# A list-scheduled transformer block: the scheduler's durations, tails and semaphore latencies set to figures read from a profile

## The chip, the cores and the metric

Each kernel runs on one core of a Trainium2 chip. Runs 1 to 4 below were taken on one chip, 5 to 8 on a second and 9 to 12 on a third, each time with the kernel before in the same rounds (medians 871.2, 870.7 and 871.7). The time is device microseconds (us) from the first to the last instruction, the median of several executions. All runs compared here are of the fast state. Ratios are the mean time of one kernel's fast runs over the mean of the other's of the same rounds, so they are not quite the ratio of the medians quoted. A profile is one execution; its span is 1 to 3 us shorter than the time of the run.

The clock granted to PE varies a little among runs of the fast state, and the time goes with it: in the rounds of runs 1 to 4 the kernel before took 869.85 to 870.05 us at a mean clock of 1.000 and 877.17 at 0.987. Most runs below had 0.996 to 1.000, so by my estimate from these figures (7.2 us for 0.013) some 2 us of a difference between two kernels can be the clock's.

The engines in the profile's lines: PE (matrix multiplication), PEld (its weight load), ACT (ScalarE), DVE (VectorE), POOL (GpSimd).

## The reference

A transformer block on 2048 tokens of width 512: layer norm, attention with 32 heads of 16, a residual, layer norm, a gated feed-forward part of width 1792, a residual.

```python
h  = x + mha(layernorm(x), wqkv, wo)           # 32 heads, Dh = 16, softmax over 2048 keys
h2 = h + (gelu(n @ w_gate) * (n @ w_up)) @ w_down      # n = layernorm(h)
```

Attention dominates: 2048 tiles of scores, 128 keys by 512 query columns each, and each needs an exponential (759.2 of ACT's 803.3 busy us in the profile of before, and DVE's conversions another 275.4 on DVE).

## The kernel before

All instructions are put in order when the program is built. Each part of the work (scores, exponentials, products with V, projections, feed-forward) is a stream of operations with a planned duration. A greedy scheduler keeps a clock for each engine and always emits the operation that can start first by that clock. Each engine gets its own list of instructions in that order, with semaphores for the true dependences. So by design a planned duration can't make a wrong result (two experiments, 8 and 12, did give one, with the look-ahead and the tail reserve moved); it only changes order, and one choice described below.

When may an operation start, by the plan?

```python
            if op.eng == "pe":
                lag = LAT + (SLACK if op.writes[0] in SOFT else 0.0)      # LAT = 0.12
                return max([self.done[t] + lag for t in toks if t[0] != "pe"] + [0.0])
            ...
            self.done[tok] = end + (PLAG if op.mode != "f" else 0.0)      # PLAG = 0.02
```

The exponential of a tile can be had in two ways. ACT takes two tiles per instruction (1024 columns, two banks of `pbank`, double-buffered):

```python
            yield Op("act", 0.093 + 0.427 * n, ACTF(PT[...], pbank[:, b0:b0 + n, :], ACT.Exp, ...), ...)
```

DVE takes single tiles. It converts each one to 16 bits, and finishes a group of four with two bit operations and one product:

```python
    def dconv(G, j, b):
        yield Op("dve", 0.7, lambda e: e.tensor_scalar(out=dXE..., in0=pbank[:, b, :], ...), ...)
    def dchain(G):
        t1, t2 = 0.16 + 0.133 * n, 0.16 + 0.267 * n      # n = 4 tiles
        yield Op("dve", t1, ...)                         # W: mantissa
        yield Op("dve", t1, ...)                         # E: exponent
        yield Op("dve", t2, ...)                         # product
```

A tile has no fixed engine. While the program is built, a new DVE group is opened whenever the plan of DVE is less than 0.8 us ahead (and the ring of four buffers has room, and 3 us have passed):

```python
        def room():
            if C["gopen"] or ... or sch.t["dve"] > sch.now + 0.8:
                return False
            ...
            return sch.now >= C["dnext"] + (DBUSY if C["down"] < first_t[C["cdone"]] else 0)
```

So planned durations decide how many tiles DVE gets. That is the one choice besides order.

Dense matmuls (projections, feed-forward) go between the scores, if they end no later than a limit before the next scores are due:

```python
        due = self.due = max(q[0][0], self.t["act"] - QLEAD)              # QLEAD = 0.5
        ok = [... if s.head.mode == "q" or max(self.t["pe"], r) + s.head.dur + ... <= due + QTOL]   # QTOL = 0.2
```

## Time and profile before

| | before |
|---|---|
| time, median (range) | 871.05 us (870.17 to 871.24, 4 runs) |
| span of the profile | 869.4 us |
| ACT exponentials / DVE conversions | 816 / 417 |

The prediction below shows the page's main lines. Here are the lines behind one term of its account: a visit of ACT to the gelu table, in order of time (start, duration, engine, line, operation, tiles).

```profile
307.07 1.28 ACT L1809 ACT_TABLE_LOAD   x1
308.37 6.27 ACT L1809 ACTIVATE GUT<-GUT 128x3584 bf16<-128x3584 bf16 x2
314.65 1.28 ACT L1278 ACT_TABLE_LOAD   x1
315.95 7.56 ACT L1278 ACTIVATE PT<-pbank 128x1024 bf16<-128x1024 f32 x8
```

From the first load to the next exponential: 315.95 - 307.07 = 8.88 us in which ACT makes no exponential. Such a visit isn't idle time, so it must be a term of its own.

The waits (who waited for whom: us in total, times, longest):

```profile
DVE dXE L1590 <- PE pbank L1272: 58.9, 122, 1.4
...
ACT PT L1278 <- PE pbank L1272: 22.4, 32, 9.0
PEld pbank L1272 <- DVE dXE L1590: 15.4, 47, 0.4
```

DVE waits four times as long for PE as PE's scores and products wait for DVE's conversions: DVE has room. The third line is the one to watch when DVE is filled.

### The profile page before, as it was taken

Reading aid. Unit: us, or ns where it says so; the run is one execution under the profiler, and the core shown is the slowest. Engines: PE = TensorE matmul, PEld = TensorE weight load, DVE = VectorE, ACT = ScalarE, POOL = GpSimd, SP = SyncE. Lnnn points to the kernel's source line nnn. Section 1 sums busy time; section 2 is a strip of 40 time slices with the busy share of each in tenths; the row PEclk is TensorE's granted clock in tenths of the full one; section 3 lists DMA queues with packets and bytes.
Section 4 is the critical chain, followed back from the end, with each engine's and each line's share of the span. In section 5 each row is a group of like instructions: output and inputs, shape, how many; then the busy total and the mean of one; then the engine's idle time right before and its main releaser. Section 6 shows DMA issues by size and latency. Waiting matters only on the chain.

```text
span 869.4 us, 16682 instructions
## 1 busy us (share of the span) xinstructions
PE 840.3 (97%) x6781; PEld 255.7 (29%) x6781; DVE 735.0 (85%) x1177; ACT 803.3 (92%) x853; POOL 42.2 (5%) x100
## 2 busy tenths in 40 slices
PE   8999999999999989999999989999999989999987
PEld 4222222222222222222222222222233333334445
DVE  7669999999879989899988989889888898589842
ACT  2799999999999999999999999999999999999941
POOL 4700000000010000000020000000000000000000
PEclk9999999999999999999999999999999999999999
DMA  6000005200000000000000000000000000000000
GB/s 194 1 1 1 1 2 199 69 1 2 2 12 1 2 1 1 13 25 2 1 13 2 1 1 1 13 26 1 1 26 2 2 1 2 8 26 8 2 13 18
DMA packets 12328, 15.06 MB, mean 17 GB/s; under 512 B 1745, under 2 KB 11217, under 8 KB 12241
## 3 DMA queue, kind: packets, MB, share of 16 engines
q1 hardware_dynamic: 12240, 13.90, 4.8%
q8 instruction: 55, 0.90, 0.4%
q14 instruction: 33, 0.26, 0.1%
HBM read 11.80 MB, written 2.10 MB: 16 GB/s over the span
## 4 chain that ended last, share of the span: by engine, by line
PE 70%; ACT 20%; issue 6%; DVE 3%; POOL 0%; ACTq 0%; DVEq 0%; POOLq 0%
PE pbank L1272 43%; PE pbank L1271 20%; ACT PT L1278 18%; PE pbank L1870 4%; ACT GUT L1809 1%; PE pbank L1867 1%; PE pbank L1275 1%; ACT L1278 1%; PE pbank L1880 1%; DVE VA L1428 1%; PE pbank L1747 0%; DVE stats L1344 0%; DVE dXE L1590 0%; PE pbank L1725 0%; DVE QT L1416 0%
## 5 line engine op out<-in xcount | busy, mean ns | idle before, releaser
L1278 ACT ACTIVATE PT<-pbank 128x1024 bf16<-128x1024 f32 x816 | 759.2, 1077 | 24.8 <-PE pbank L1272 22.4
L1272 PE MATMUL pbank<-QT,KT 32*128 32x512 bf16 x2048 | 349.5, 384 | 11.1 <-ACT PT L1278 9.3
L1590 DVE TENSOR_SCALAR dXE<-pbank 128x512 uint16<-128x512 f32 x417 | 275.4, 686 | 62.0 <-PE pbank L1272 58.9
L1272 PEld LDWEIGHTS pbank<-QT,KT 32*128 32x128 bf16 x2048 | 83.4, 91 | 325.8 <-ACT PT L1278 239.1
L1272 PE MATMUL pbank<-PT,VA 128*17 128x512 bf16 (+1 forms) x2045 | 150.8, 338 | 0.0
L1607 DVE TENSOR_TENSOR dXE<-dW,dXE 128x2048 f16<-128x2048 f16 (+1 forms) x105 | 127.3, 1212 | 1.6
L1604 DVE TENSOR_SCALAR dW<-dXE 128x2048 uint16<-128x2048 uint16 (+1 forms) x105 | 71.7, 683 | 1.6
L1870 PE MATMUL pbank<-ones_bf,zero_bf 128*128 128x512 bf16 x220 | 72.4, 386 | 0.0
L1605 DVE TENSOR_SCALAR dXE<-dXE 128x2048 uint16<-128x2048 uint16 (+1 forms) x105 | 71.5, 681 | 0.0
L1271 PE MATMUL pbank<-hnT_c,wg_sb 128*128 128x512 bf16 (+1 forms) x280 | 66.5, 344 | 0.0
L1272 PE MATMUL pbank<-dXE,VA 128*17 128x512 f16 (+1 forms) x1030 | 64.2, 341 | 0.0
L1271 PE MATMUL pbank<-hnT_c,wu_sb 128*128 128x512 bf16 (+1 forms) x280 | 58.3, 338 | 5.9 <-DVE GUT L1823 5.9
L1271 PE MATMUL pbank<-wd_sb,GUT 128*128 128x512 bf16 x224 | 60.1, 382 | 0.0
L1272 PEld LDWEIGHTS pbank<-PT,VA 128*17 128x17 bf16 x2045 | 39.3, 88 | 66.5 <-issue 60.9
L1823 DVE TENSOR_TENSOR GUT<-pbank,GUT 128x512 bf16<-128x512 f32 x56 | 37.1, 685 | 10.2 <-PE pbank L1271 9.5
L1741 POOL TENSOR_SCALAR rstd<-mv 128x1 f32<-128x1 f32 x16 | 5.8, 361 | 784.4 <-DVE mv L1739 784.4
L1271 PE MATMUL pbank<-xnT,wqkv_sb 128*128 128x512 bf16 x128 | 37.7, 384 | 0.2 <-DVE dXE L1590 0.2
L1797 DVE CAST GUT<-pbank 128x512 bf16<-128x512 f32 x49 | 33.2, 683 | 1.9 <-PE pbank L1271 1.4
L1271 PEld LDWEIGHTS pbank<-hnT_c,wu_sb 128*128 128x128 bf16 x280 | 22.9, 98 | 31.2 <-issue 10.3
L1271 PEld LDWEIGHTS pbank<-hnT_c,wg_sb 128*128 128x128 bf16 x280 | 20.1, 99 | 27.8 <-issue 21.1
L1870 PEld LDWEIGHTS pbank<-ones_bf,zero_bf 128*128 128x128 bf16 x220 | 15.3, 97 | 35.5 <-issue 35.1
L1272 PEld LDWEIGHTS pbank<-dXE,VA 128*17 128x17 bf16 x1030 | 16.6, 88 | 27.3 <-issue 19.8
(82 smaller groups left out, 400.1 us busy)
## 6 DMA issues: line engine op xcount, KB each, us to landing
xres<-in_A_x_dram SPq DMA_DIRECT2D x16, 128.0 KB, 2.2
out_dram<-out_sb SPq DMA_DIRECT2D x16, 128.0 KB, 1.7
wg_sb<-in_B_w_gate_dram SPq DMA_DIRECT2D x1, 1792.0 KB, 7.1
wu_sb<-in_B_w_up_dram SPq DMA_DIRECT2D x1, 1792.0 KB, 11.3
wd_sb<-in_B_w_down_dram SPq DMA_DIRECT2D x1, 1792.0 KB, 17.4
x_sb<-in_A_x_dram SPq DMA_DIRECT2D x3, 512.0 KB, 8.3
wqkv_sb<-in_A_wqkv_dram SPq DMA_DIRECT2D x1, 896.0 KB, 7.5
x_sb<-in_A_x_dram SPq DMA_DIRECT2D x2, 256.0 KB, 2.9
```

Source lines behind the costliest of these rows:

```text
L1271: return lambda e: e.matmul(o, l, r, start=start, stop=stop)
L1272: return lambda e: e.matmul(o, l, r, start=start, stop=stop, tile_position=tile)
L1275: return lambda e: e.transpose(out=o, in_=i, identity=idn)
L1278: return lambda e: e.activation(out=o, in_=i, func=func, **kw)
L1428: op = Op("dve", 0.61, lambda e, b=b, t=t: e.tensor_copy(out=VA[:, t, :, 0:16], in_=pbank[:, b, :].rearrange("p (h i) -> p h i", i=16)), r ...
L1590: yield Op("dve", 0.7, lambda e: e.tensor_scalar(out=dXE[G["k"] % NX][:, 0, j, :], in0=pbank[:, b, :], scalar1=XMIN + 1024.0 * CENTER, sca ...
L1604: yield Op("dve", t1, lambda e: e.tensor_scalar(out=W.bitcast(U16), in0=X, scalar1=0x3ff, scalar2=0xb800, op0=ALU.bitwise_and, op1=ALU.bit ...
L1605: yield Op("dve", t1, lambda e: e.tensor_scalar(out=E, in0=X, scalar1=0x7c00, scalar2=0x8, op0=ALU.bitwise_and, op1=ALU.bitwise_or), reads ...
L1607: yield Op("dve", t2, lambda e: e.tensor_tensor(out=X.bitcast(F16), in0=W, in1=X.bitcast(F16), op=ALU.mult), reads=kW + kX, writes=kX, por ...
L1797: yield Op("dve", 0.68, lambda e: e.tensor_copy(out=o_ap, in_=i_ap), reads=[("pb", b)], writes=keys, extra=dE)
L1823: yield Op("dve", 0.69, lambda e: e.tensor_tensor(out=o_ap, in0=u_ap, in1=o_ap, op=ALU.mult), reads=[("pb", b)] + keys, writes=keys)
L1870: fill_op = Op("pe", TMM, lambda e: e.matmul(pbank[:, PVB, :], zero_bf[:], ones_bf[:], start=False, stop=False, skip_group_check=True), re ...
```

## The change

Its intent: make the scheduler's clock agree with the chip's. No instruction changes its kind or size. There are five parts: DVE's durations; ACT's exponential and its other durations; PE's durations; a tail for each engine and a latency for each pair of engines in place of a single 0.12 us; the allowance for dense work. (A tail is how far the reported end of an instruction reaches past the next one's start, most often 0.083 us on DVE in the trace of before; a latency is the time from the reported end of an instruction to the start of the one waiting for it, there most often 34 ns from DVE to DVE and 52 ns from ACT to PE's weight load.) (The new `TUNIT` only scales the deadlines that rank the streams; set back alone, it builds a program with the same 796 exponentials and 456 conversions, and it was not run on the chip.) Cut to its core:

```diff
-            if op.eng == "pe":
-                lag = LAT + (SLACK if op.writes[0] in SOFT else 0.0)
-                return max([self.done[t] + lag for t in toks if t[0] != "pe"] + [0.0])
-            lag = LAT + (SLACK if op.eng == "act" and op.writes[0][0] == "w" else 0.0)
-            return max([self.done[t] + lag for t in toks] + [self.port if op.port else 0.0])
+            lag = SLACK if (op.eng == "pe" and op.writes[0] in SOFT) or (op.eng == "act" and op.writes[0][0] == "w") else 0.0
+            return max([self.done[t] + LATS.get((t[0], op.eng), LAT) + lag for t in toks if t[0] != "pe" or op.eng != "pe"] + [self.port if op.port else 0.0])
...
-            self.done[tok] = end + (PLAG if op.mode != "f" else 0.0)
+            self.done[tok] = end + TAIL.get(op.eng, 0.0)
...
-TMM, TTR, TTR32, TST = 0.225, 0.11, 0.26, 0.213
-TSW, PLAG = 0.1, 0.02
+TMM, TTR, TST = 0.217, 0.056, 0.213
+TSW = 0.105
+TEXP = lambda n: 0.062 + 0.427 * n
+TAIL = dict(pe=0.17, act=0.13, dve=0.083)
+LATS = {("pe", "act"): 0.04, ("pe", "dve"): 0.04, ("act", "pe"): 0.058, ("dve", "pe"): 0.06, ("dve", "dve"): 0.034, ("act", "act"): 0.04, ("pool", "pool"): 0.05}
...
-QLEAD = 0.5
-QTOL = 0.2
+QLEAD = 0.43
+QTOL = 0.1
...
-    TUNIT = 0.88 * 64 * (0.093 * len(SLOTS) / sum(n for _, n in SLOTS) + 0.427)
+    TUNIT = 0.8 * 64 * sum(TEXP(n) for _, n in SLOTS) / sum(n for _, n in SLOTS)
...
-            yield Op("act", 0.093 + 0.427 * n, ACTF(PT[:, p0:p0 + n, :], pbank[:, b0:b0 + n, :], ACT.Exp, ...
+            yield Op("act", TEXP(n), ACTF(PT[:, p0:p0 + n, :], pbank[:, b0:b0 + n, :], ACT.Exp, ...
...
-        yield Op("dve", 0.7, lambda e: e.tensor_scalar(out=dXE[G["k"] % NX][:, 0, j, :], ...
+        yield Op("dve", 0.603, lambda e: e.tensor_scalar(out=dXE[G["k"] % NX][:, 0, j, :], ...
...
-        t1, t2 = 0.16 + 0.133 * n, 0.16 + 0.267 * n
+        t1, t2 = 0.07 + 0.133 * n, 0.066 + 0.267 * n
...
-        yield Op("dve", 0.68, lambda e: e.tensor_copy(out=OA[:, par, :], ...       # and 22 more durations of DVE and ACT
+        yield Op("dve", 0.6, lambda e: e.tensor_copy(out=OA[:, par, :], ...
```

More of the change, by code (lines that the diff above doesn't have):

```diff
@@ L978, in _emit @@
         for tok in extra:
-            start = max(start, self.done[tok] + LAT)
+            start = max(start, self.done[tok] + LATS.get((tok[0], op.eng), LAT))
         self.now = max(self.now, start)
@@ L1327, in ln1 @@
             for t in sa:
-                yield Op("act", 0.82, lambda e, t=t: e.activation(out=sqj[:], in_=x_sb[:, t, :], func=ACT.Copy, accum_out=hsum[:, t:t + 1]),
+                yield Op("act", 0.52, lambda e, t=t: e.activation(out=sqj[:], in_=x_sb[:, t, :], func=ACT.Copy, accum_out=hsum[:, t:t + 1]),
                          reads=[xkey(c, t)], writes=["sqj", ("hsum", t)])
-                yield Op("act", 0.82, lambda e, t=t: e.activation(out=sqj[:], in_=x_sb[:, t, :], func=ACT.Square, accum_out=hsq[:, t:t + 1]),
+                yield Op("act", 0.52, lambda e, t=t: e.activation(out=sqj[:], in_=x_sb[:, t, :], func=ACT.Square, accum_out=hsq[:, t:t + 1]),
                          reads=[xkey(c, t)], writes=["sqj", ("hsq", t)])
@@ L1343, in ln1 @@
             if t not in sa:
-                yield Op("dve", 0.66, lambda e, t=t: e.bn_stats(out=stats[:, t, :], in_=x_sb[:, t, :]), reads=[xkey(c, t)], writes=[("stats", t)])
-                yield Op("dve", 0.15, lambda e, t=t: e.bn_aggr(out=mv[:, t, :], in_=stats[:, t, :]), reads=[("stats", t)], writes=[("mv", t)])
+                yield Op("dve", 0.605, lambda e, t=t: e.bn_stats(out=stats[:, t, :], in_=x_sb[:, t, :]), reads=[xkey(c, t)], writes=[("stats", t)])
+                yield Op("dve", 0.1, lambda e, t=t: e.bn_aggr(out=mv[:, t, :], in_=stats[:, t, :]), reads=[("stats", t)], writes=[("mv", t)])
                 sch.add(ln1_rstd(t), 2 + 7 * c)
@@ L1359, in ln1_norm @@
         if c < 2:
-            yield Op("dve", 0.35,
+            yield Op("dve", 0.327,
                      lambda e: e.tensor_scalar(out=xn_sb[:, t % 8, :], in0=x_sb[:, t, :], scalar1=mv[:, t, 0:1], scalar2=rstd[:, tt_], op0=ALU.subtract, op1=ALU.mult),
@@ L1379, in ln1_T @@
         o_ap, i_ap = xnT[:, :, 128 * t:128 * t + 128], pt[:, 0:512].rearrange("p (c s) -> p c s", c=4)
-        yield Op("dve", 0.42, lambda e: e.tensor_copy(out=o_ap, in_=i_ap), reads=[("pb", b)], writes=[("xnT", t)])
+        yield Op("dve", 0.333, lambda e: e.tensor_copy(out=o_ap, in_=i_ap), reads=[("pb", b)], writes=[("xnT", t)])
         sch.release(b)
@@ L1405, in k_evac @@
     def k_evac(j, c, b, dl):
-        yield Op("dve", 0.61, lambda e: e.tensor_copy(out=KT[:, j, 512 * c:512 * c + 512], in_=pbank[:, b, :]), reads=[("pb", b)], writes=[("kT", j, c)])
+        yield Op("dve", 0.605, lambda e: e.tensor_copy(out=KT[:, j, 512 * c:512 * c + 512], in_=pbank[:, b, :]), reads=[("pb", b)], writes=[("kT", j, c)])
         proj_done(b)
@@ L1412, in q_evac @@
             if par == 0 and dl < T0:
-                yield Op("act", 0.6, lambda e: e.activation(out=QT[:, c, 2 * j, :], in_=pbank[:, b, :], func=ACT.Copy, scale=qmask[:, 0:1]),
+                yield Op("act", 0.47, lambda e: e.activation(out=QT[:, c, 2 * j, :], in_=pbank[:, b, :], func=ACT.Copy, scale=qmask[:, 0:1]),
                          reads=[("pb", b), ("qm", 0)], writes=[("qT", 2 * j, c)])
             else:
-                yield Op("dve", 0.61, lambda e, par=par: e.tensor_scalar(out=QT[:, c, 2 * j + par, :], in0=pbank[:, b, :], scalar1=qmask[:, par:par + 1], scalar2=None, op0=ALU.mult),
+                yield Op("dve", 0.66, lambda e, par=par: e.tensor_scalar(out=QT[:, c, 2 * j + par, :], in0=pbank[:, b, :], scalar1=qmask[:, par:par + 1], scalar2=None, op0=ALU.mult),
                          reads=[("pb", b), ("qm", par)] + [("qT", 2 * j, c)] * par, writes=[("qT", 2 * j + par, c)])
@@ L1427, in proj_v @@
                                       for dc in (2 * hf, 2 * hf + 1)], reads=rd, writes=[("pb", b)])
-            op = Op("dve", 0.61, lambda e, b=b, t=t: e.tensor_copy(out=VA[:, t, :, 0:16], in_=pbank[:, b, :].rearrange("p (h i) -> p h i", i=16)),
+            op = Op("dve", 0.605, lambda e, b=b, t=t: e.tensor_copy(out=VA[:, t, :, 0:16], in_=pbank[:, b, :].rearrange("p (h i) -> p h i", i=16)),
                     reads=[("pb", b)], writes=[("V", t)])
@@ L1514, in exps @@
             p0, n = an % NRING, len(mine)
-            yield Op("act", 0.093 + 0.427 * n, ACTF(PT[:, p0:p0 + n, :], pbank[:, b0:b0 + n, :], ACT.Exp, scale=LN2 / 1024, bias=math.log(PSCALE)),
+            yield Op("act", TEXP(n), ACTF(PT[:, p0:p0 + n, :], pbank[:, b0:b0 + n, :], ACT.Exp, scale=LN2 / 1024, bias=math.log(PSCALE)),
                      reads=[("pb", b0 + k) for k in range(n)], writes=[("PT", p0 + k) for k in range(n)],
@@ L1589, in dconv @@
     def dconv(G, j, b):
-        yield Op("dve", 0.7, lambda e: e.tensor_scalar(out=dXE[G["k"] % NX][:, 0, j, :], in0=pbank[:, b, :], scalar1=XMIN + 1024.0 * CENTER, scalar2=XMIN, op0=ALU.add, op1=ALU.max),
+        yield Op("dve", 0.603, lambda e: e.tensor_scalar(out=dXE[G["k"] % NX][:, 0, j, :], in0=pbank[:, b, :], scalar1=XMIN + 1024.0 * CENTER, scalar2=XMIN, op0=ALU.add, op1=ALU.max),
                  reads=[("pb", b)], writes=[("dX", G["k"] % NX, j)], gate=lambda: C["gpv"] >= G["k"] - NX + 1 and (G["k"] % NX < NX - 1 or C["ln1"] == NT), extra=dE if G["k"] % NX == NX - 1 else None)
@@ L1673, in ofin @@
         nb = CHUNKS[c] // 128
-        yield Op("dve", 0.68, lambda e: e.tensor_copy(out=OA[:, par, :], in_=pbank[:, PVB, :]), reads=[("pb", PVB)], writes=[("OA", par)])
+        yield Op("dve", 0.6, lambda e: e.tensor_copy(out=OA[:, par, :], in_=pbank[:, PVB, :]), reads=[("pb", PVB)], writes=[("OA", par)])
         C["oa"] = u + 1
@@ L1680, in ofin @@
         li = LINV[:, u, :].rearrange("p (q g) -> p q g", g=4)
-        yield Op("dve", 0.2, lambda e: e.reciprocal(out=li, in_=pt[:, 0:512].rearrange("p (q g i) -> p q g i", q=4, g=4)[:, :, :, 16]), reads=[("pb", b)], writes=[("LINV", u)])
+        yield Op("dve", 0.165, lambda e: e.reciprocal(out=li, in_=pt[:, 0:512].rearrange("p (q g i) -> p q g i", q=4, g=4)[:, :, :, 16]), reads=[("pb", b)], writes=[("LINV", u)])
         for x, slot in enumerate(slots):
@@ L1686, in ofin @@
             o_ap = Otok[:, cp, 0:nb, 128 * j:128 * j + 128].rearrange("p q (g x i) -> p q g x i", g=4, x=2)[:, :, :, par_, :]
-            yield Op("dve", 0.1 + 0.26 / len(slots), lambda e, o4=o4, lx=lx, o_ap=o_ap: e.tensor_tensor(out=o_ap, in0=o4[:, :, :, 0:16], in1=lx.unsqueeze(3).broadcast_to([128, nb, 4, 16]), op=ALU.mult),
+            yield Op("dve", 0.06 + 0.28 / len(slots), lambda e, o4=o4, lx=lx, o_ap=o_ap: e.tensor_tensor(out=o_ap, in0=o4[:, :, :, 0:16], in1=lx.unsqueeze(3).broadcast_to([128, nb, 4, 16]), op=ALU.mult),
                      reads=[("pb", b), ("LINV", u)], writes=[("Otok", cp, slot)])
@@ L1714, in copy_op @@
         if c == NC - 1 and qt % 2:
-            return Op("act", 0.6, lambda e: e.activation(out=o, in_=i, func=ACT.Copy), **kw)
-        return Op("dve", 0.42, lambda e: e.tensor_copy(out=o, in_=i), **kw)
+            return Op("act", 0.47, lambda e: e.activation(out=o, in_=i, func=ACT.Copy), **kw)
+        return Op("dve", 0.333, lambda e: e.tensor_copy(out=o, in_=i), **kw)
     def post(c, qt):
@@ L1733, in post @@
         dQ = P.retire(h_over[c])
-        yield Op("dve", 0.61, lambda e: e.tensor_tensor(out=hh[:, qt, :], in0=pbank[:, b2, :], in1=xres[:, xi, :], op=ALU.add),
+        yield Op("dve", 0.605, lambda e: e.tensor_tensor(out=hh[:, qt, :], in0=pbank[:, b2, :], in1=xres[:, xi, :], op=ALU.add),
                  reads=[("pb", b2), ("xres", xi)], writes=[("h", c, qt)], extra=lambda: dQ)
@@ L1737, in post @@
         C["oproj"] += 1
-        yield Op("dve", 0.66, lambda e: e.bn_stats(out=stats2[:, t, :], in_=hh[:, qt, :]), reads=[("h", c, qt)], writes=[("stats2", t)])
+        yield Op("dve", 0.605, lambda e: e.bn_stats(out=stats2[:, t, :], in_=hh[:, qt, :]), reads=[("h", c, qt)], writes=[("stats2", t)])
         yield Op("dve", 0.1, lambda e: e.bn_aggr(out=mv2[:, t, :], in_=stats2[:, t, :]), reads=[("stats2", t)], writes=[("mv2", t)])
@@ L1742, in post @@
         yield Op("pool", 0.57, lambda e: e.tensor_tensor(out=rstd2[:, tt_], in0=rstd2[:, tt_], in1=nhalf[:, 0:1], op=ALU.pow), reads=[("rstd2", t), "nhalf"], writes=[("rstd2", t)])
-        yield Op("dve", 0.35, lambda e: e.tensor_scalar(out=hn_sb[:, qt, :], in0=hh[:, qt, :], scalar1=mv2[:, t, 0:1], scalar2=rstd2[:, tt_], op0=ALU.subtract, op1=ALU.mult),
+        yield Op("dve", 0.327, lambda e: e.tensor_scalar(out=hn_sb[:, qt, :], in0=hh[:, qt, :], scalar1=mv2[:, t, 0:1], scalar2=rstd2[:, tt_], op0=ALU.subtract, op1=ALU.mult),
                  reads=[("h", c, qt), ("rstd2", t), ("mv2", t)], writes=[("OH", qt)], port=True)
@@ L1792, in gate_evac @@
         if c == NC - 1:
-            yield Op("act", 0.55, lambda e: e.activation(out=o_ap, in_=i_ap, func=ACT.Gelu_apprx_tanh), reads=[("pb", b)], writes=keys)
+            yield Op("act", 0.47, lambda e: e.activation(out=o_ap, in_=i_ap, func=ACT.Gelu_apprx_tanh), reads=[("pb", b)], writes=keys)
             sch.release(b)
@@ L1796, in gate_evac @@
             return
-        yield Op("dve", 0.68, lambda e: e.tensor_copy(out=o_ap, in_=i_ap), reads=[("pb", b)], writes=keys, extra=dE)
+        yield Op("dve", 0.6, lambda e: e.tensor_copy(out=o_ap, in_=i_ap), reads=[("pb", b)], writes=keys, extra=dE)
         sch.release(b)
@@ L1808, in gelu @@
             keys = [("GUT", f) for f in range(f0, f1)]
-            yield Op("act", 0.2 + 0.000833 * nq * (f1 - f0) + TTAB * (hf == 0) + TTAB * (hf == GSPLIT - 1), lambda e, ap=ap: e.activation(out=ap, in_=ap, func=ACT.Gelu_apprx_tanh), reads=keys, writes=keys)
+            yield Op("act", 0.05 + 0.000833 * nq * (f1 - f0) + TTAB * (hf == 0) + TTAB * (hf == GSPLIT - 1), lambda e, ap=ap: e.activation(out=ap, in_=ap, func=ACT.Gelu_apprx_tanh), reads=keys, writes=keys)
             for k in range(f0 // pack(c), f1 // pack(c)):
@@ L1822, in up_evac @@
         u_ap = pbank[:, b, :].rearrange("p (f q) -> p f q", f=pack(c))
-        yield Op("dve", 0.69, lambda e: e.tensor_tensor(out=o_ap, in0=u_ap, in1=o_ap, op=ALU.mult), reads=[("pb", b)] + keys, writes=keys)
+        yield Op("dve", 0.6, lambda e: e.tensor_tensor(out=o_ap, in0=u_ap, in1=o_ap, op=ALU.mult), reads=[("pb", b)] + keys, writes=keys)
         sch.release(b)
@@ L1839, in down_evac @@
         oi = t % 2
-        yield Op("dve", 0.65, lambda e: e.tensor_tensor(out=out_sb[:, oi, :], in0=pbank[:, b, :], in1=h_c[c][:, qt, :], op=ALU.add),
+        yield Op("dve", 0.6, lambda e: e.tensor_tensor(out=out_sb[:, oi, :], in0=pbank[:, b, :], in1=h_c[c][:, qt, :], op=ALU.add),
                  reads=[("pb", b), ("h", c, qt)], writes=[("osb", oi)])
```

## The prediction

> **What bounds the kernel now.** I read the page's engine shares and slices first, then busy time by stretch, then the costliest groups, then the stream of ACT and of DVE in order of time, last the waits.
>
> ```profile
> PE 840.3 (97%) x6781; PEld 255.7 (29%) x6781; DVE 735.0 (85%) x1177; ACT 803.3 (92%) x853; POOL 42.2 (5%) x100
> ACT  2799999999999999999999999999999999999941
> ```
>
> The page makes PE look fullest. But a matmul's end is modelled and matmuls overlap[...]. ACT's row is the one to follow: nearly full in 36 of 40 slices, empty only at the two ends. By stretch (PE, PEld, DVE, ACT, POOL busy):
>
> ```profile
> 100.00:200.00 100.00, 99.19 (x750) 24.71 (x744) 93.49 (x139) 99.74 (x110) 0.00 (x0) 1.00 0.17 59
> 400.00:500.00 100.00, 98.14 (x745) 25.44 (x742) 89.55 (x145) 99.02 (x108) 5.40 (x8) 1.00 0.01 4
> ```
>
> The groups say what ACT and DVE do. The scores of 2048 tiles go to an exponential: ACT takes two tiles per instruction (1024 columns), DVE takes the rest one by one, then finishes them by fours (two bit operations and a product).
>
> ```profile
> L1278 ACT ACTIVATE PT<-pbank 128x1024 bf16<-128x1024 f32 x816 | 759.2, 1077 | 24.8 <-PE pbank L1272 22.4
> L1590 DVE TENSOR_SCALAR dXE<-pbank 128x512 uint16<-128x512 f32 x417 | 275.4, 686 | 62.0 <-PE pbank L1272 58.9
> L1607 DVE TENSOR_TENSOR dXE<-dW,dXE 128x2048 f16<-128x2048 f16 (+1 forms) x105 | 127.3, 1212 | 1.6
> ```
>
> 815 x 2 + 1 + 417 = 2048. So the split between ACT and DVE is what sets the time: an ACT step fewer is worth a step's spacing. That spacing isn't the mean of 1077 ns in the row, because one instruction's end overlaps the next. Reading the starts:
>
> ```profile
> 27.40 3.77 ACT L1278 ACTIVATE PT<-pbank 128x1024 bf16<-128x1024 f32 x4 [8.98 <-PE pbank L1272]
> 99.02 77.67 ACT L1278 ACTIVATE PT<-pbank 128x1024 bf16<-128x1024 f32 x84 [0.31 <-PE pbank L1272]
> 832.08 1.28 ACT L1846 ACT_TABLE_LOAD   x1
> ```
>
> (3.77 - 1.077) / 3 = 0.898 and (77.67 - 1.077) / 83 = 0.923. Over all 811 neighbouring pairs of exponentials the smallest distance between starts is 0.903 us, and more than half sit there: that is ACT unhindered. The account of the 869.4 us: 17.4 to the first exponential; 816 x 0.903 = 736.8 unhindered; four visits to the gelu table, 8.9 + 8.9 + 8.9 + 5.9 = 32.5; 37.3 from the end of the last exponential (832.06) to the end; the remaining 45.4 is ACT held up. Of that one hole of 9.0 is at the start (the line above with 8.98). From 50 to 830 us I find 143 steps spaced more than 40 ns over 0.903, together 32.6 us. In most, PE ran dense matmuls (gate and down projections lead) just before the scores that ACT needed.
>
> DVE in order of time:
>
> ```profile
> 401.03 0.68 DVE L1674 CAST OA<-pbank 128x512 bf16<-128x512 f32 x1
> 401.63 0.68 DVE L1604 TENSOR_SCALAR dW<-dXE 128x2048 uint16<-128x2048 uint16 x1
> 402.23 0.69 DVE L1605 TENSOR_SCALAR dXE<-dXE 128x2048 uint16<-128x2048 uint16 x1
> 402.83 1.29 DVE L1590 TENSOR_SCALAR dXE<-pbank 128x512 uint16<-128x512 f32 x2
> ```
>
> Instructions of 0.68 to 0.69 start 0.60 apart: the last 0.083 of each lies under the next. Taking 0.083 from each of DVE's instructions leaves 700 us of occupied time, 84 to 88% in most stretches of 50 us, though busy time shows 90. So DVE has room. The waits agree: DVE waits 58.9 us for PE before the conversions.
>
> [...]DVE starts 34 ns after the end of the DVE instruction it waits for, PE's weight load about 52 after ACT's end.[...]
>
> **The change, part by part.** No instruction changes its kind or size. The program is ordered when it is built, by a greedy list scheduler that keeps a clock for each engine, and the change alters that clock. So the time changes only through the order, and through how many tiles the scheduler gives to DVE.
>
> 1. DVE's planned cost. It opens a group of four tiles whenever its plan of DVE is less than 0.8 us ahead. Old plan of one group: 4 x 0.70 + 2 x (0.16 + 0.133 x 4) + (0.16 + 0.267 x 4) = 5.41 us. New: 4 x 0.603 + 2 x 0.602 + 1.134 = 4.75. The trace's distances (conversion 0.60, bit operations 0.60, product 1.13) say 4.75 is right. Now 417 x 0.603 + 105 x 2.338 = 497 of DVE's 700 us are group work; the other 203 were planned about 16 us too long (evacuations 0.68 for 0.60, copies 0.42 for 0.33). Old planned load: 417 x 0.70 + 105 x 2.612 + 219 = 785. Old planned length of ACT: 815.5 x (0.093 + 0.854 = 0.947) + 33 = 805. That is 97.5%: by its plan DVE was full.
>
> 2. ACT's planned cost falls too, 0.947 to 0.916. With G groups there are 1024 - 2G steps. If the planner fills DVE to the same 97.5%: 203 + 4.75 G = 0.975 x (0.916 x (1024 - 2G) + 32.5), so 6.54 G = 743 and G = 114, against 104.25 now. ACT steps: 796 for 815.5, some 19.5 fewer, x 0.903 = 17.6 us less. The same sum by stretch of 50 us gives 113 to 114.
>
> 3. Hold-ups of ACT. Old plan: a dense operation may end up to 0.947 - 0.5 + 0.2 = 0.65 after the exponential that frees the bank; new: 0.916 - 0.43 + 0.1 = 0.59. After it come a switch (0.1), the scores (0.213), the tail and the semaphore (0.21): 1.17 against 1.11, where ACT is ready at 0.903. The worst planned delay falls from 0.27 to 0.21. On 32.6 us that fifth is 6 or 7 us; but the same dense work must fit into fewer steps, so I take 4.
>
> 4. The ends. Transposes are planned at 0.056 for 0.11, normalization statistics at 0.605 for 0.66; ACT's statistics go to 0.52 (start to next start with the accumulator read is about 0.76, so this got worse). The hole of 9 us may shrink or move; I take 0. After the last exponential the chain of 37 us is dependent work; I take 0.
>
> Sum: 871.0 - 17.6 - 4 = about 849.
>
> **The rivals.** (a) DVE becomes the bound. The plan will put 203 + 4.75 x 114 = 745 us on DVE in about 795: 94%, and it plans ACT 1.4% slower than ACT is. Now 14% of slack absorbs every late arrival; then 3 to 6% would. PE waits in order for DVE to free a bank (15.4 us for conversions before scores and products now), so late DVE would stall scores and ACT. For it: the slack does go. Against it: the times and latencies are now right, so the plan sees most such waits. It would give back 5 to 15 us: 855 to 865. (b) The number of groups is capped by something other than DVE (ring of four buffers, 3 us between openings, at least one group still not multiplied): G stays near 106 and only order changes: 860 to 869. Against: a group every 7.9 us now, far from 3, and the planned load was 97.5%. (c) The better plan removes much more: most of the 32.6 us and part of the hole, with 118 groups: 832 to 838. (d) The clock of PE: [...]granted clock is 1.00 until 800 us. No effect.
>
> **Range and chances.** Rival (a) partly present and (c) partly present spread the sum by some 9 us each way, a little more upward: 838 to 863. The line of 2% lies at 871.0 x 0.98 = 853.6, only 5 us above the sum, so faster 0.65, same 0.32, slower 0.03.
>
> **What would show it.** Step 1 and 2: the conversions rise from 417 to about 455 and the ACT exponentials fall from 816 to about 797; DVE's mean durations stay at 686 and 1212 ns, its busy share rises above 88%. Step 3: unhindered spacing still 0.903, sum of hold-ups outside the start under 33 us. Step 4: first exponential near 17 us, last one to the end near 37. If conversions don't rise, step 2 is wrong and (b) holds; if they rise and those waits of PE on DVE grow well beyond 15 us, (a) holds; if the time after the last exponential grows, the end was misjudged.

## The result, and the profile after

844.37 us (844.12 to 844.89, 4 runs) against 871.05: ratio 0.9696, 95% interval 0.968 to 0.9713. Faster by 3.0%; the prediction said 849 within 838 to 863.

The page of the changed kernel, the same two lines:

```profile
PE 819.5 (97%) x6773; PEld 254.4 (30%) x6773; DVE 769.0 (91%) x1246; ACT 786.3 (93%) x833; POOL 42.9 (5%) x100
ACT  3979999999999999999999999999999999999941
```

DVE went from 85% to 91% and executes 69 instructions more; ACT executes 20 fewer. PE's share didn't move. It is not the row to steer by: its matmuls overlap (ten of 0.38 us each that start at 857.89 us in the profile of before take 2.33 us together), and 267 of them before and 203 after only multiply a tile of zeros (87.9 and 66.8 us). The same stretches as before:

```profile
100.00:200.00 100.00, 97.73 (x758) 25.25 (x751) 98.95 (x152) 99.33 (x109) 0.00 (x0) 1.00 0.17 59
...
400.00:500.00 100.00, 96.29 (x733) 25.45 (x732) 96.04 (x156) 99.44 (x104) 3.13 (x8) 1.00 0.01 4
```

In the second stretch DVE's busy time (the third engine) is 96.0 for 89.6, at the same 99% of ACT. Now both are nearly full. The groups:

```profile
L1278 ACT ACTIVATE PT<-pbank 128x1024 bf16<-128x1024 f32 x796 | 742.3, 1072 | 17.7 <-PE pbank L1272 14.6
...
L1590 DVE TENSOR_SCALAR dXE<-pbank 128x512 uint16<-128x512 f32 x456 | 296.9, 682 | 15.9 <-PE pbank L1272 12.8
...
L1607 DVE TENSOR_TENSOR dXE<-dW,dXE 128x2048 f16<-128x2048 f16 (+1 forms) x115 | 139.1, 1210 | 2.0
```

456 conversions for 417 and 796 exponentials for 816. The mean durations are the same (682 for 686, 1210 for 1212, 1072 for 1077): nothing got faster, the work was dealt out differently. Idle time before the conversions fell from 62.0 to 15.9 us. The waits:

```profile
PEld pbank L1272 <- DVE dXE L1590: 18.3, 50, 0.5
ACT PT L1278 <- PE pbank L1272: 14.6, 27, 2.9
...
DVE dXE L1590 <- PE pbank L1272: 12.8, 35, 1.0
```

DVE's wait for PE shrank from 58.9 to 12.8; PE's wait for DVE grew by 3 us only. ACT's longest wait for scores went from 9.0 to 2.9. Where that was, in ACT's order of time:

```profile
17.00 1.02 ACT L1278 ACTIVATE PT<-pbank 128x1024 bf16<-128x1024 f32 x1 [2.08 <-PE pbank L1272]
18.92 11.21 ACT L1278 ACTIVATE PT<-pbank 128x1024 bf16<-128x1024 f32 x12 [0.89 <-PE pbank L1272]
```

The hole between the first and the second exponential, 9 us before, is 0.9. Part of it seems to have moved: waits of up to 1.6 us now come between 30 and 44 us, where ACT had none before.

**The account.** I use one for all kernels. The span is the time to the first exponential, plus steps x 0.903 (a step is one ACT exponential, 0.903 the smallest distance between two starts, the same in the two profiles), plus the visits to the gelu table between exponentials, plus the hold-ups of ACT (the remainder between first and last exponential), plus the end from the last exponential on.

| us | first | steps x 0.903 | gelu | hold-ups | end | span |
|---|---|---|---|---|---|---|
| before | 17.4 | 816: 736.8 | 32.5 | 45.3 | 37.3 | 869.4 |
| after | 17.0 | 796: 718.8 | 32.5 | 39.1 | 35.7 | 843.2 |
| difference | -0.4 | -18.0 | 0 | -6.2 | -1.6 | -26.2 |

Two thirds come from 20 fewer steps. Of the hold-ups, the starts that come late in the first 50 us sum to 9.2 before and 5.0 after; later delays of over 40 ns sum to 32.6 before and 30.1 after.

Two of the small differences may be the clock's in part, and not the plan's. In the profile of before, the granted clock fell to 0.87 from 840 to 844 us and to 0.70 from 844 to 848, inside the end; in that of after it was 1.00 from 808 to 840. So the 1.6 us at the end can't be put down to the change. In the profile of after, the clock was 0.50 from 501 to 504 us, and ACT then waited 1.05 us at 505.58.

### The profile page after: what moved, and what is told of

It is laid out like the page before. It is cut to its first block, busy times and chain, and to the rows that moved or that the text cites. A ratio compares the mean times of both kernels' runs of the same rounds, so it can differ in the third digit from the quotient of the medians.

```text
span 843.2 us, 16693 instructions
## 1 busy us (share of the span) xinstructions
PE 819.5 (97%) x6773; PEld 254.4 (30%) x6773; DVE 769.0 (91%) x1246; ACT 786.3 (93%) x833; POOL 42.9 (5%) x100
## 4 chain that ended last, share of the span: by engine, by line
PE 75%; ACT 12%; DVE 6%; issue 5%; POOL 1%; ACTq 0%; POOLq 0%; DVEq 0%
PE pbank L1272 46%; PE pbank L1271 21%; ACT PT L1278 11%; PE pbank L1870 3%; DVE dXE L1590 2%; DVE dXE L1607 1%; PE pbank L1275 1%; ACT GUT L1809 1%; PE pbank L1867 1%; PE pbank L1880 1%; DVE dXE L1605 1%; POOL xn_sb L1369 1%; DVE dW L1604 1%; PE pbank L1725 0%; PE pbank L1747 0%
## 5 line engine op out<-in xcount | busy, mean ns | idle before, releaser
L1278 ACT ACTIVATE PT<-pbank 128x1024 bf16<-128x1024 f32 x796 | 742.3, 1072 | 17.7 <-PE pbank L1272 14.6
L1272 PE MATMUL pbank<-QT,KT 32*128 32x512 bf16 x2048 | 345.0, 384 | 7.2 <-ACT PT L1278 4.9
L1590 DVE TENSOR_SCALAR dXE<-pbank 128x512 uint16<-128x512 f32 x456 | 296.9, 682 | 15.9 <-PE pbank L1272 12.8
L1607 DVE TENSOR_TENSOR dXE<-dW,dXE 128x2048 f16<-128x2048 f16 (+1 forms) x115 | 139.1, 1210 | 2.0
L1604 DVE TENSOR_SCALAR dW<-dXE 128x2048 uint16<-128x2048 uint16 (+1 forms) x115 | 78.1, 679 | 0.8
L1605 DVE TENSOR_SCALAR dXE<-dXE 128x2048 uint16<-128x2048 uint16 (+1 forms) x115 | 78.1, 679 | 0.0
L1272 PE MATMUL pbank<-dXE,VA 128*17 128x512 f16 (+1 forms) x1136 | 70.3, 339 | 0.0
L1870 PE MATMUL pbank<-ones_bf,zero_bf 128*128 128x512 bf16 x168 | 55.7, 386 | 0.0
L1823 DVE TENSOR_TENSOR GUT<-pbank,GUT 128x512 bf16<-128x512 f32 x56 | 37.3, 685 | 16.0 <-PE pbank L1271 12.8
L1271 PEld LDWEIGHTS pbank<-hnT_c,wu_sb 128*128 128x128 bf16 x280 | 23.5, 99 | 32.5 <-issue 11.8
L1272 PEld LDWEIGHTS pbank<-dXE,VA 128*17 128x17 bf16 x1136 | 18.7, 88 | 29.8 <-issue 24.0
L1271 PEld LDWEIGHTS pbank<-wd_sb,GUT 128*128 128x128 bf16 x224 | 17.0, 97 | 27.0 <-issue 14.3
## 6 DMA issues: line engine op xcount, KB each, us to landing
wd_sb<-in_B_w_down_dram SPq DMA_DIRECT2D x1, 1792.0 KB, 17.4
```

The lines of the kernel that those rows point to most:

```text
L1271: return lambda e: e.matmul(o, l, r, start=start, stop=stop)
L1272: return lambda e: e.matmul(o, l, r, start=start, stop=stop, tile_position=tile)
L1278: return lambda e: e.activation(out=o, in_=i, func=func, **kw)
L1590: yield Op("dve", 0.603, lambda e: e.tensor_scalar(out=dXE[G["k"] % NX][:, 0, j, :], in0=pbank[:, b, :], scalar1=XMIN + 1024.0 * CENTER, s ...
L1604: yield Op("dve", t1, lambda e: e.tensor_scalar(out=W.bitcast(U16), in0=X, scalar1=0x3ff, scalar2=0xb800, op0=ALU.bitwise_and, op1=ALU.bit ...
L1605: yield Op("dve", t1, lambda e: e.tensor_scalar(out=E, in0=X, scalar1=0x7c00, scalar2=0x8, op0=ALU.bitwise_and, op1=ALU.bitwise_or), reads ...
```

## The experiments

The question is which of the new figures does it, and why a DVE filled to 94% doesn't hold up ACT. (Occupied time of DVE from 100 to 700 us, each instruction less its last 0.083 us: 85.9% before, 93.7% after.) Four kernels come first: parts of the change alone, or undone. Each diff is against the kernel named; in kernels built from before, lines after the constants stand three numbers lower down (L1281 for L1278, L1593 for L1590).

**1. DVE's durations alone.** Before, plus:

```diff
-        yield Op("dve", 0.7, ...dXE...)
+        yield Op("dve", 0.603, ...dXE...)
-        t1, t2 = 0.16 + 0.133 * n, 0.16 + 0.267 * n
+        t1, t2 = 0.07 + 0.133 * n, 0.066 + 0.267 * n
 # and the change's other DVE durations
```

> The kernel before, with the change's durations of DVE's operations alone; ACT, PE and all latencies are planned as before. The built program has 796 ACT exponentials for 816. Theory (the share of tiles sets the time, a step is worth 0.903 us): 20 x 0.903 = 18 us less, so 853; hold-ups of ACT stay near the 45 us of before (42 to 48). Rival (a fuller DVE only pays with right latencies and PE times): late DVE gives half or more back, 860 to 869, with hold-ups above 52.

855.42 us (855.39 to 855.96), ratio 0.9802 to before (0.975 to 0.9855). The account of its profile: 17.1 + 718.8 + 32.5 + hold-ups 50.3 + 35.4 = 854.1. So the count of steps is that of the changed kernel, and gives its 18 us of the account; but 5 us of hold-ups are added, where the changed kernel lost 6. Its waits:

```profile
PEld pbank L1275 <- DVE dXE L1593: 29.9, 80, 0.7
ACT PT L1281 <- PE pbank L1275: 22.9, 40, 6.3
DVE dXE L1593 <- PE pbank L1275: 14.7, 34, 1.3
```

PE waits 29.9 us for DVE's conversions, 15.4 before and 18.3 in the changed kernel. The rival (late DVE holds up ACT) is there, at a part of the size that it had claimed.

**2. Everything but DVE's durations.** After, with the old DVE durations.

```diff
-        yield Op("dve", 0.603, ...dXE...)
+        yield Op("dve", 0.7, ...dXE...)
-        t1, t2 = 0.07 + 0.133 * n, 0.066 + 0.267 * n
+        t1, t2 = 0.16 + 0.133 * n, 0.16 + 0.267 * n
 # and the other DVE durations of before
```

> The changed kernel with the old durations of DVE's operations. The built program has 816 ACT exponentials, as before. Theory (share): only the 8 us that did not come from the share remain (hold-ups 45 to 39, end 37 to 36): 863, within 860 to 866. Rival (the order by right latencies and PE times is the main part): 846 to 855 at 816 steps.

867.98 us (867.35 to 868.66, 20 runs), ratio 0.9952 (0.9939 to 0.9966). 816 steps, hold-ups 44.0, end 35.8. This is above the 860 to 866 that I expected: without the new share, the better order gains 3 us, not 8. So the hold-ups that the changed kernel lost, it lost only together with the new share. The first two runs give 16 and 3 us alone; both together give 27. The remaining 8 us came only with the combination.

**3. Old latencies and tails.** After, with the first hunk of the diff and the line with `TAIL` undone.

```diff
-            self.done[tok] = end + TAIL.get(op.eng, 0.0)
+            self.done[tok] = end + (PLAG if op.mode != "f" else 0.0)
 # and the single LAT = 0.12 in _ready and _emit
```

> The changed kernel with the old latencies (one figure of 0.12 us for all, hardly a tail). The built program has 800 exponentials for 796. Theory (share, latencies matter little): 844.4 + 4 x 0.903 = 848, hold-ups near 39. Rival (right tails and latencies are what keeps a full DVE from holding up ACT): hold-ups above 47 us and 855 or more.

847.09 us (846.75 to 847.74), as the share alone says (848). 800 steps, hold-ups 37.9. Tails and latencies, the most laborious part of the change, are worth 4 steps here and no hold-ups.

**4. Old durations of PE.** After, with:

```diff
-TMM, TTR, TST = 0.217, 0.056, 0.213
-TSW = 0.105
+TMM, TTR, TTR32, TST = 0.225, 0.11, 0.26, 0.213
+TSW, PLAG = 0.1, 0.02
```

> The changed kernel with the old times of PE (matmul 0.225 for 0.217, transpose 0.11 for 0.056, switch 0.1 for 0.105). The built program has 801 exponentials for 796. Theory (share): 844.4 + 5 x 0.903 = 849. Rival (the smaller planned PE times are what let dense work fit between the scores): hold-ups 45 or more, 855 or more.

851.32 us (850.67 to 853.63). 801 steps, hold-ups 38.7; the last visit to the gelu table fell behind the last exponential (gelu 26.6, end 41.9). Five steps are 4.5 us, and the hold-ups are those of the changed kernel: not PE's durations either.

What is left is the exponential's own planned duration, 0.916 for 0.947, the allowance, and ACT's other durations. Looking at runs 1 and 2 and the two kernels, a new theory offers itself. By the plan DVE is filled to the brim. If the plan takes ACT to be slower than it is, a DVE that is full by the plan is more than full at ACT's real pace, and ACT must wait for it. In run 1 DVE is planned truly and ACT at 0.947 / 0.903 = 1.05 of its real spacing. The old kernel made both errors at once: its DVE group was planned at 5.41 / 4.75 = 1.14 of its real cost, which hid the other.

**5. DVE's durations and the exponential's, nothing else.** Run 1 plus:

```diff
-            yield Op("act", 0.093 + 0.427 * n, ...Exp...)
+            yield Op("act", TEXP(n), ...Exp...)      # 0.062 + 0.427 * n
```

> The kernel before with the change's durations of DVE and of ACT's exponential (0.916 for 0.947), nothing else. 802 exponentials. In the run with DVE's durations alone ACT was held up 50 us, in the changed kernel 39, at 796 steps in both. Theory A (that run's extra 11 us come from planning ACT slower than it is, so that DVE, planned full, can't keep its pace): hold-ups 37 to 42, so 802 x 0.903 = 724 + 17 + 32.5 + 39 + 35.5 + 1 = 849. Theory B (the latencies or PE's lead do it): hold-ups 48 or more, 858 or more.

847.66 us (846.21 to 847.77), ratio 0.9728 (0.9693 to 0.9763). 802 steps, hold-ups 35.3 for 50.3 in run 1. The last visit to the gelu table fell behind the last exponential, as in run 4 (gelu 26.6, end 41.8; together 68.4, for 67.9 in run 1). DVE is about as full (92.9% for 93.2%), with 445 conversions for 457. Its waits:

```profile
PEld pbank L1275 <- DVE dXE L1593: 22.5, 63, 0.4
...
ACT PT L1281 <- PE pbank L1275: 13.0, 20, 2.1
```

That is what theory A said; these two durations give some 23 of the change's 27 us. As DVE got 12 tiles less too, a lighter load on it isn't excluded by this run alone; the next one excludes it.

**6. The changed kernel with the old exponential.**

```diff
-TEXP = lambda n: 0.062 + 0.427 * n
+TEXP = lambda n: 0.093 + 0.427 * n
```

> The changed kernel with the old duration of the exponential in the plan (0.947). 793 exponentials. Theory A (the true pace of ACT in the plan keeps hold-ups at 39): hold-ups 48 to 52, 716 + 17 + 32.5 + 50 + 35.5 + 1 = 852. Theory B (it is something else): hold-ups near 39 and 841.

857.89 us (857.18 to 859.83). 793 steps, three fewer than the changed kernel, and 13 us slower: hold-ups 52.9, a little above the 48 to 52 that I gave, and the time 6 us above my 852. DVE is filled as in the changed kernel (93.9% for 93.7%), so the load on DVE is not the difference.

```profile
PEld pbank L1272 <- DVE dXE L1590: 26.0, 77, 0.8
ACT PT L1278 <- PE pbank L1272: 20.6, 58, 2.7
```

A reader who minimizes the count of steps would choose this kernel over the changed one.

**7. The old allowance.** After, with:

```diff
-QLEAD = 0.43
-QTOL = 0.1
+QLEAD = 0.5
+QTOL = 0.2
```

> The changed kernel with the old allowance for dense work ahead of the scores (lead 0.5 and tolerance 0.2 for 0.43 and 0.1). 799 exponentials. My prediction's third step (the allowance shortens each late start, worst case 0.27 to 0.21 us): hold-ups after 50 us rise by 4 to 7 us to 34 to 37, so 844.4 + 2.7 + 5 = 852. Rival (the allowance is not what delays ACT): hold-ups as in the changed kernel, 847.

851.11 us (850.88 to 851.82). 799 steps; hold-ups 41.3, of them after 50 us 32.7 (30.1 in the changed kernel). So the allowance is worth 2.6 us there, on one profile each: the sign that my prediction gave, but below the 4 to 7 that I expected of this run. The time came out near my 852 all the same: three more steps are 2.7 us, and the first exponential came 0.5 later.

**8. Planning constants moved, found by a search for fewer steps and an earlier end of the plan.** After, with:

```diff
-LOOK = 0.12
+LOOK = 0.06
-ATAIL = 8
-AWIN = 16
+ATAIL = 12
+AWIN = 20
```

> The changed kernel with three planning constants moved (look-ahead 0.06 us for 0.12, window of candidates 20 for 16, tail reserve 12 for 8). 789 exponentials for 796. Share theory: 7 x 0.903 = 6.3 less, 838. Rival (DVE has no room left at 94% and gives it back): 843 to 848 with hold-ups of 44 or more.

845.89 us, and the result is wrong (relative error 0.028), so it is no candidate. As a time it agrees with the rival: 789 steps, hold-ups 45.3, DVE at 95.4%. Of the error I can only say that the count of products is complete (1577 tiles of ACT's and 942 products of DVE's 471 tiles, two each); its cause stays open (see run 12).

**9 and 10. DVE's group work planned at 0.9 and at 1.1 of what it takes.** After, with:

```diff
 # run 9
-        yield Op("dve", 0.603, ...dXE...)
+        yield Op("dve", 0.543, ...dXE...)
-        t1, t2 = 0.07 + 0.133 * n, 0.066 + 0.267 * n
+        t1, t2 = 0.063 + 0.1197 * n, 0.059 + 0.2403 * n
 # run 10
+        yield Op("dve", 0.663, ...dXE...)
+        t1, t2 = 0.077 + 0.1463 * n, 0.073 + 0.2937 * n
```

> The changed kernel with DVE's group work planned at 0.9 of what it takes. 784 exponentials for 796, so the plan gives DVE more than it can do at ACT's pace. Theory A (what counts is that planned paces of ACT and DVE are both true; a DVE planned too fast by x holds up ACT): the two runs with ACT planned 5% too slow had hold-ups of 50 and 53, so here 55 to 65 and 708 + 17 + 32.5 + 60 + 36 + 1 = 854, slower than the changed kernel in spite of 12 steps fewer. Share alone (a step is a step): 12 x 0.903 = 11 less, 833.

866.88 us (866.2 to 867.63, 6 runs), ratio 0.9932. 784 steps, 12 fewer than the changed kernel, and 22 us slower. Hold-ups 72.2: the direction of theory A, and more than the 55 to 65 that I gave it. Its waits, where the one of PE for DVE is three times that of the changed kernel:

```profile
PEld pbank L1272 <- DVE dXE L1590: 53.9, 127, 1.0
ACT PT L1278 <- PE pbank L1272: 34.3, 83, 2.1
```

> The other side: DVE's group work planned at 1.1 of what it takes. 813 exponentials. Theory A: DVE has slack again, hold-ups 38 to 44 as in the run with the old DVE durations (44), so 734 + 17 + 32.5 + 41 + 36 + 1 = 862. If slack on DVE were worth much by itself, hold-ups would fall to 30 or less and 850.

859.68 us (856.67 to 862.38). The spread goes roughly with the granted clock: 856.67 at 0.999, 859.78 at 0.996, 859.59 at 0.993 and 862.38 at 0.991; the profile is of the fastest run. It has 813 steps, hold-ups 34.7, lower than the 38 to 44 that I expected, and DVE waits for PE again:

```profile
DVE dXE L1590 <- PE pbank L1272: 39.2, 88, 1.6
...
PEld pbank L1272 <- DVE dXE L1590: 13.5, 42, 0.4
```

**11. The exponential planned at the spacing that the trace shows.** After, with:

```diff
-TEXP = lambda n: 0.062 + 0.427 * n
+TEXP = lambda n: 0.049 + 0.427 * n      # 0.903 for two tiles
```

> The changed kernel with the exponential planned at 0.903 us, the spacing that the trace shows, for 0.916. 801 exponentials for 796. Theory A: the last 1.4% of wrong pace goes, hold-ups fall from 39 to 33 to 36, and the five more steps cost 4.5: 844 within 2, so no gain. If pace below 2% doesn't matter: hold-ups 39, 849.

840.66 us (840.27 to 841.03), ratio 0.964 (0.961 to 0.967). Five steps more than the changed kernel, and still faster than it: hold-ups 31.9. I had expected 33 to 36 and no gain. Its waits:

```profile
PEld pbank L1272 <- DVE dXE L1590: 21.3, 61, 0.5
...
ACT PT L1278 <- PE pbank L1272: 11.3, 21, 2.7
```

Not all of the gain is hold-ups: here too the last gelu visit came after the last exponential, and gelu and end together take 66.2 us for 68.2 in the changed kernel. The result is correct, and this is the fastest correct kernel of the study. It ran in other rounds than the changed kernel; compared through the kernel before, 0.964 / 0.9696 is 0.6% less, by the medians 0.4%, and its clock was a little higher (0.999 to 1.000 for 0.997 to 0.998).

**12. A try to beat both.** After, with:

```diff
-TEXP = lambda n: 0.062 + 0.427 * n
+TEXP = lambda n: 0.053 + 0.427 * n
-LOOK = 0.12
-ATAIL = 8
+LOOK = 0.09
+ATAIL = 10
```

> A try to beat both: the exponential planned at 0.907 us, look-ahead 0.09 for 0.12 us, tail reserve 10 tiles for 8. 794 exponentials. By theory A hold-ups 33 to 36: 717 + 17 + 32.5 + 34 + 36 + 1 = 838, 6 us under the changed kernel. Rival (the schedule is as good as its order allows, 39 held up): 843.

832.23 us, hold-ups 30.7 at 794 steps (the last gelu visit again behind the last exponential), but the result is wrong again (relative error 0.028). Runs 8 and 12 both move the look-ahead and the tail reserve and no other run does, so one of these is the likely trigger. Whether an order that they make breaks a dependence that the kernel doesn't declare was not tried. Nothing faster than run 11 can be claimed.

**What the late steps waited for.** The sums of waits above include waits that delay no exponential. So the steps spaced more than 40 ns over 0.903 after the first 50 us were split by one question, asked of the kept traces: between the starts of the two exponentials, did a weight load of PE wait for an instruction of DVE? The lateness of the steps where it did, and of the others:

| kernel | late steps with such a wait: us | the others: us |
|---|---|---|
| before | 16.5 | 16.2 |
| 1 | 23.5 | 16.5 |
| 5 | 9.7 | 15.4 |
| after | 12.1 | 18.0 |
| 6 | 21.4 | 22.6 |
| 9 | 35.9 | 26.9 |
| 11 | 6.0 | 18.0 |

From run 1 to 5, 13.8 of the 14.9 us that are gained lie in steps with such a wait; from the changed kernel to run 6, 9.3 of 13.9; from it to run 11, 6.1 of 6.1. So what a wrong pace brings in is, for the larger part, steps in which PE waited for DVE; steps late for other reasons, dense matmuls among them, hardly change between runs 1 and 5 or the changed kernel and run 11, and take the smaller part of the rise in runs 6 and 9. In the kernel before, half of the lateness was already of this kind.

**The runs in one row.** "Pace" is the planned over the real cost of a DVE group, divided by the planned over the real spacing of ACT: how much dearer the plan takes DVE to be, relative to ACT, than it is. Example, run 1: (4.75 / 4.75) / (0.947 / 0.903) = 0.95. The table has the runs that moved it, and the two kernels.

| kernel | pace | steps | hold-ups, us | PE's wait for DVE's conversions, us |
|---|---|---|---|---|
| 9 | 0.89 | 784 | 72.2 | 53.9 |
| 6 | 0.95 | 793 | 52.9 | 26.0 |
| 1 | 0.95 | 796 | 50.3 | 29.9 |
| after | 0.99 | 796 | 39.1 | 18.3 |
| 5 | 0.99 | 802 | 35.3 | 22.5 |
| 11 | 1.00 | 801 | 31.9 | 21.3 |
| 10 | 1.08 | 813 | 34.7 | 13.5 |
| before | 1.09 | 816 | 45.3 | 15.4 |

Below 1 the hold-ups rise steeply: from run 11 to run 9, 17 steps fewer (15 us gained) cost 40 us of waiting. Above 1 they don't go on falling, and the steps rise. Among the correct kernels the time is shortest where the pace is 1. The last column doesn't order the runs as the hold-ups do (run 11 has more of these waits than the changed kernel, and fewer hold-ups); the split above does better. Pace isn't all: runs 3, 4 and 7, with the pace of the changed kernel, have hold-ups of 37.9, 38.7 and 41.3, but run 8 (whose result is wrong), with the same pace and 789 steps, has 45.3. Run 2 lies at 5.41 / 4.75 / 1.014 = 1.12 with hold-ups of 44.0, so above 1 there is more to it than pace, and that part isn't settled.

## Why the prediction was right

**Right: the bound and the share.** ACT's stream of exponentials sets the time, and the planner filled DVE to the same degree as before. The balance gave 114 groups and 796 to 797 steps, and the trace shows 115 groups, 456 conversions (455 predicted) and 796 steps. The term was -17.6 us; measured -18.0. Runs 1 and 2 show it from both sides. The other signs came too: DVE's means at 682 and 1210 ns, its busy share at 91%, the smallest spacing at 0.903, the first exponential at 17.0. Hold-ups after the start under 33 us came as well (30.1), but they were 32.6 before, so that sign could tell little.

**Mis-sized: the hold-ups and the ends.** I took -4 for hold-ups and 0 for the rest. The hold-ups fell by 6.2, the end by 1.6, the time to the first exponential by 0.4, together 8.2 for 4. That is the difference between 849 and 844.4. And the 4 were put in the wrong place: most of the fall is at the start (9.2 to 5.0), for which step 4 took 0; the later delays fell by 2.5. The allowance, my reason for it, is worth about that much (run 7). So that the term came near is partly luck: the start, which I left out, gave more than it, and the end's share may be partly the clock's. Step 3 also laid the late steps to dense matmuls and missed that half of their lateness had a wait for DVE beside it (16.5 of 32.6).

**Half seen: rival (a).** I argued that a DVE filled to 94% would lose its slack, and that right times and latencies would protect it. (That 14% of slack absorbed every late arrival was an estimate; 16.5 of the 32.6 us late had a wait for DVE beside them.) The outcome agrees with that, but the reason was too broad. With the old latencies the hold-ups were 37.9 us (run 3), with PE's old durations 38.7 (run 4), for 39.1 in the changed kernel. What protects a full DVE is a true duration of the exponential in the plan: 52.9 us with 0.947 (run 6). I treated its fall from 0.947 to 0.916 as a small loss in step 2, since a faster ACT leaves fewer tiles for DVE. Run 6 shows that with the old figure the changed kernel would be at 858, a gain of half the size. I did note that ACT was still planned 1.4% slower than it is, and listed it as a risk; run 11, without it, is about 4 us faster, of which some 2 us are in the last gelu visit and the end.

**Refuted: rivals (b) and (c).** Conversions rose to 456, and to 480 in run 9, so nothing but DVE's plan capped them near 417. (c) needed 118 groups and far fewer hold-ups; neither came with the change.

**Rival (d), the clock:** the mean granted clock is 0.997 in both profiles, so it doesn't make the 26 us. That it has no effect was my estimate; in the rounds of runs 1 to 4 the kernel before took 869.85 us at 1.000 and 877.17 at 0.987.

## What to carry to other kernels

In a planner that divides work between two engines, take both costs as distances between starts, not as the durations that the profile lists (here 0.903 for 1.077 us on ACT, 0.60 for 0.68 on DVE), and check their ratio first: planning the exponential 5% too long in place of 1.4% cost 13 us (run 6), all tails and latencies 3 us (run 3). A plan that made one engine's share larger than it could carry showed in the trace as waits of the engine between the two (in run 9 PE waited 53.9 us for DVE's conversions, 18.3 in the changed kernel), and the count of instructions on the bound engine then misled (784 steps for 796, and 22 us slower). If two planned costs are both too high, correct them together; correcting DVE's alone gave 16 of 27 us. The exponential's alone was not run.
